# How the negated score maxima get from partitions into rows, and where early score tiles stand, in a fused layernorm, attention and gated MLP kernel

## The chip, the cores and the metric

One core of one Trainium2 chip runs the whole kernel as a single program. The metric is device time in microseconds, from the program's start to its end. The kernel before took 1572.92 us in the median of three runs (1572.62 to 1572.99).

The engines are named as the profile names them. PE is TensorE (PEld is its weight load, which overlaps its products), DVE is VectorE, ACT is ScalarE, POOL is GpSimd, and SP is SyncE, which here only issues DMAs. SPq and PEq are the instruction queues of SP and PE.

## What is computed

The input `x` has 2048 tokens of 512 features. All is float32.

```python
xn = layernorm(x)
q, k, v = split(xn @ wqkv)              # 32 heads of 16 features
scores = einsum("bhqd,bhkd->bhqk", q, k) * 16 ** -0.5
p = softmax(scores, axis=-1)
s = einsum("bhqk,bhkd->bhqd", p, v).reshape(1, 2048, 512) @ wo
g = silu(gelu(xn @ w1 + b1) @ w2 + b2)  # 1376 hidden features
out = x + s * g
```

The softmax subtracts each row's maximum, so every query of every head needs the maximum of its 2048 scores before its exponentials are taken. This study is about the way of these maxima through the kernel.

## The kernel before

**Precision.** Products are made in float32r, and where full accuracy is needed an operand is split into a high part and a low rest, so that one product becomes three (high by high, high by low, low by high). The attention scores do this inside one product: the 48 rows of a K tile and of a Q tile hold the 16 features of a head three times, as high, high and low, against high, low and high.

**Units and steps.** The attention is cut into 32 units: 8 groups of 4 heads by 4 chunks of 512 queries; unit `u` has group `u // 4` and chunk `u % 4`. A unit has 16 steps, one for each 128 keys, so there are 512 steps (the loop of line 975). A step is a short program of letters, `ORDER` and `AFTER` (lines 40 and 41), most often `TSXTTSTYV`:

- T (`t_one`, line 709) is the score tile of one head, 128 keys by 512 queries. Its product has 50 rows: the 48 of the features and two more, in which the K side holds ones and the Q side, `QT[u]`, holds the negated maxima as a high and a low part. So the maximum is subtracted inside the product (line 716). ACT takes the exponential from PSUM (line 718). A step has four Ts, and their PSUM banks come from `t_tile` (line 701): three of `ps_t` and the one of `ps_m` in turn.
- V (`pv_step`, line 775) multiplies the exponentials of the step before by V; a column of ones in V gives the sums. After a unit's sixteenth step DVE copies the result out (line 788).
- S, X and Y are score tiles made only for their maxima, 128 queries by 512 keys, for a unit that comes later. Their banks are a ring of three in the attention (two before it). DVE takes the maxima of each half of 256 keys (line 190). X and Y are the two halves of a tile cut in two.

**The early phase.** Before the attention, layernorm, the projections of Q, K and V and the MLP are computed. Most of it is a list called `plan`, whose products run on two halves of the PE array, 64 rows each: `run` (line 595) takes two lists of products and issues them in turn, one for the upper and one for the lower rows. Ahead of each product it calls `fill(a)` (line 564), which may put in one early score tile. `LEAD = 144` makes 576 early score tiles, the maxima of units 0 to 8; they use the banks `ps_a` and `ps_b` in turn. A tile of half `a` is due when the row counter of that half, which counts products and early tiles of that half, reaches

```python
due = FILL0 + put[0] + sum(made) * ROWS // (4 * LEAD)    # line 565; ROWS is 1728, so 3 for each tile made
```

Since the two halves have counters of their own and take turns, the tiles stand seven products apart, then three, then seven.

**How a unit's maxima are finished.** After 64 tiles `s_end0` (line 239) joins the maxima of all key parts: `nm` holds, for 128 queries on the partitions, 16 negated maxima (4 heads by 4 query tiles) (line 248, DVE). `s_max` (line 187) calls it right after the reduction of the next score tile, so in the attention it stands where that tile happens to stand in its step. POOL makes the high and the low part (lines 251 and 252) into `nmh`. The maxima now lie on the partitions, one query on each, and have to become rows of `QT[u]`. For this a product with the identity transposes them into PSUM (`s_end1`, line 268), for two units at once up to unit 27 and for one unit at a time after it (`PAIRED`, line 43). Its bank is one of the score tiles' ring in the early phase and one of the T ring in the attention, but for the last unit. A copy brings it to SBUF (`s_end2`: ACT in the early phase, line 276, DVE in the attention, line 278), and SP writes it to DRAM (line 279) as `mh_d`, in which a head's 512 maxima are one run. `load_mh` (line 149) then reads them with two DMAs of 8 KB, each into two rows of `QT[u]`.

`tick`, `flush` and the list `later` count score tiles or steps until line 268 is put in (12 in the early phase, 8 in the attention, where a step counts four).

**Order of the work around it.** All orders are written out by hand (`manual_schedule`): an engine runs its instructions in the order in which the Python code makes them. `at(n, ...)` (line 925) puts an operation into step `n`. Unit `u`'s rows of Q are loaded at step `16 * u - 14`, and `load_mh` stands at that step too, or four steps after the unit's pair has all its tiles if that is later (two steps for the last unit) (lines 944 to 946). `o_move` and `o_den` (lines 798 and 807), which carry a finished unit's result and sums, stand on the same SP queue. SP's DMAs share eight completion semaphores in turn, so each waits until the one eight before it has landed.

Of the kernel before, what the change touches and what calls it, by code (L numbers as in the profile page):

```python
# [8 lines left out]
F32 = mybir.dt.float32  # L9
F32R = mybir.dt.float32r  # L10
# [39 lines left out]
def fused(ctx: ExitStack, tc: tile.TileContext, x, wqk, wv, wo, w1, b1, w2, b2, out):  # L50
# [13 lines left out]
    ones_d = dpool.tile([2, S], F32, name="ones_d")  # L64
    g_d = dpool.tile([S, D], F32, name="g_d")
    den_d = dpool.tile([NG * NCH, GH, CH], F32, name="den_d")
    mh_d = dpool.tile([NG * NCH, 2, GH, CH], F32, name="mh_d")

    ident_r = keep.tile([P, P], F32R, name="ident_r")
    mhw = keep.tile([1, 1], F32, name="mhw")  # L70
# [12 lines left out]
            if then:  # L83
                then()

    QS, QT, MX, NM, MH = {}, {}, {}, {}, {}
# [62 lines left out]
    def load_mh(u):  # L149
        assert u in sent  # L150
        for a in range(2):
            nc.sync.dma_start(QT[u][64 * a + 48:64 * a + 50].bitcast(F32), mh_d[u, :, a::2, :])
# [6 lines left out]
    def units_of(u):  # L159
        return (u,) if u >= PAIRED else (u - u % 2, u - u % 2 + 1)  # L160

    def tick():
        for e in later:
# [23 lines left out]
    def s_max(ps, job, heads, parts):  # L187
        u, p = job[0], job[2]
        qi, ki = at_of(job)
        nc.vector.tensor_reduce(MX[u][:, 2 * p:2 * p + 2, qi, ki][:, heads, parts], ps.rearrange("p (n c) -> p n c", c=HC), axis=AX.X, op=OP.max)  # L190
        done[u] += 1
        if ended:
            s_end0(ended.pop())
        if done[u] == 64:
            ended.append(u)
        if done[NU - 1] == 64:
            s_end0(ended.pop())

    def s_whole(job, a):
        ps = s_tile()[0]  # L200
# [4 lines left out]
        made[a] += 1  # L205
        s_whole(heads[made[a] - 1], a)

    jobs, whole, cut, put_off = [], [], [], []

    def s_op(op):  # L210
        if op == "S":
            if whole:
                s_whole(whole.pop(), 1)
            else:
                whole.append(jobs.pop(0))
                s_whole(whole[0], 0)
        elif op == "X":
            if not cut:
                cut[:] = [jobs.pop(0), 0]
            ps, pool = s_tile(True)  # L220
            x = s_mm(ps, cut[0], 0, 0, cut[1] * HC, HC)
            cut[2:] = [ps, pool, x]
            run_off()
# [11 lines left out]
    def run_off():  # L235
        while put_off:
            put_off.pop(0)()

    def s_end0(u):
        nm = qring.tile([P, GH * NCH], F32, name="nm")  # L240
        n = len(units_of(u))
        if u == units_of(u)[0]:
            NM[u] = qring.tile([P, 2, 2, GH * NCH], F32R, name="nmh")[:, :n]
        hl = NM[units_of(u)[0]][:, u % n]
        if u == units_of(u)[-1]:
            later.append([12 if "seen" in prog else 8, units_of(u)[0]])
        mx = MX.pop(u).rearrange("p a b c n -> p (a b) (c n)")
        nc.vector.tensor_reduce(nm, mx, axis=AX.X, op=OP.max, negate=True)  # L248

        def two():  # L250
            nc.gpsimd.tensor_copy(hl[:, 0], nm)  # L251
            nc.gpsimd.tensor_sub(hl[:, 1], nm, hl[:, 0].bitcast(F32))

        put_off.append(two)
        if "seen" in prog or u == NU - 1:
            run_off()
        del QS[u]
        if "seen" in prog:
            ask_qs(u + 2)
        else:  # L260
            load_qs(u + 2)

    prog = {}

    def s_end1(u):
        pm = s_tile()[0] if "seen" in prog or u == NU - 1 else t_tile()
        n = 2 * GH * NCH * len(units_of(u))
        nc.tensor.matmul(pm[:n, :P], NM.pop(u).rearrange("p u i a -> p (u i a)"), ident_r, start=True, stop=True)
        MH[u] = pm

    def s_end2(u):
        us = units_of(u)
        n = 2 * GH * NCH * len(us)
        mh = qring.tile([4 * GH * NCH, P], F32, name="mh", bufs=1)
        if "seen" in prog:
            nc.scalar.activation(mh[:n], MH.pop(u)[:n, :P], AF.Copy)
        else:
            nc.vector.tensor_copy(mh[:n], MH.pop(u)[:n, :P])
        nc.sync.dma_start(mh_d[us[0]:us[-1] + 1].rearrange("u i j (q s) -> (u i j q) s", s=P), mh[:n])
        sent.update(us)  # L280

    sa = ExitStack()
    xp = sa.enter_context(tc.tile_pool(name="xp", bufs=1))
# [273 lines left out]

    prog.update(n=0, pe=0, seen=0)
    writer = {}
    s_when, put, row = [], [0], [0, 0]  # L560
    ndown = sum(1 for e in plan if e[0] == "down")
    ROWS = 12 * (4 * VQ + 2 * len(pairs)) + 6 * ndown - 10 + 2 * LEAD - 2 * (LEAD // 32) - FILL0

    def fill(a):
        due = FILL0 + put[0] + sum(made) * ROWS // (4 * LEAD)
        if sum(made) < 4 * LEAD and row[a] >= due and (made[0] <= made[1]) == (a == 0):
            taken()
            if later and later[0][0] <= 0:
                put[0] += 2
                u = later.pop(0)[1]  # L570
                s_end1(u)
                s_end2(u)
                return
            s_one(a)
            row[a] += 1
            tick()

    def taken():
# [5 lines left out]
    def mm(a, key, ps, lhs, rhs, first, last):  # L584
        r = slice(64 * a, 64 * a + 64)
        if not first and writer[key][0] != a and writer[key][1] > prog["seen"]:
            hold = nc.tensor.nop().ins
            tc.add_manual_dep(hold, writer[key][2], SYNC, reason="other row tile")
            prog["seen"] = writer[key][1]
        i = nc.tensor.matmul(ps, lhs[r], rhs[r], start=first, stop=last).ins  # L590
        prog["pe"] += 1
        row[a] += 1
        writer[key] = (a, prog["pe"], i.name)

    def run(ops, hooks={}):
# [335 lines left out]
    def due(n):  # L931
        return min(4 * L, 4 * LEAD + max(0, 3 * n - 1))

    for u in range(NU):
# [116 lines left out]
```

## Time and profile before

| | |
|---|---|
| median of 3 runs | 1572.92 us |
| profiled execution | 1573.31 us |
| span of its instructions | 1571.4 us |
| PE, DVE, ACT, POOL busy | 1564.2, 1397.1, 1233.8, 371.9 us |
| granted TensorE clock | 1.00 |
| layernorm and start | to about 52 us |
| early phase, two halves of the array | about 52 to 475 us |
| attention, 512 steps | about 473 to 1548 us |
| output projection, what is left of it | to the end |

The profiled execution took 1.9 us more than its span and 0.39 us more than the median. In the profile a line such as L268 is a line of the kernel before. A group gives its busy time and the mean of one instruction, and then the idle time of its engine just ahead of it and what ended that. In the timeline the first column is the start in us from the span's start and the second the duration; equal neighbours are merged (x8). In the windows each engine's busy time is followed by its number of instructions. In a DMA answer the strip is the window in 40 equal slices, each digit the share of 16 DMA engines that was busy, in tenths.

### The profile page before, as it was taken

To read this page: it belongs to the slowest core of one execution; us is meant where nothing else is said; L and a number is where in the kernel's file an instruction comes from. 1 tells how busy PE (TensorE), PEld (TensorE's weight loads), DVE (VectorE), ACT (ScalarE), POOL (GpSimd) and SP (SyncE) were. 2 spreads that over 40 slices of the span, in tenths; PEclk is the share of its full clock that TensorE was granted. 3 is DMA by queue.
4 is the path that set the end of the run, shared out by engine and by line. 5 is a ranking of instruction groups with operands and counts; after the bars stand their busy time and mean duration, and the time that the engine had idled before them with its cause. 6 is when DMAs were issued, how large, how long until landed. Compare 5 with 4: busy or idle time off the path is not lost.

```text
span 1571.4 us, 31849 instructions
## 1 busy us (share of the span) xinstructions
PE 1564.2 (100%) x12264; PEld 952.0 (61%) x12264; DVE 1397.1 (89%) x2290; ACT 1233.8 (79%) x2397; POOL 371.9 (24%) x394
## 2 busy tenths in 40 slices
PE   9999999999999999999999999999999999999998
PEld 7899999999994444444444444444444444444455
DVE  7599898989988999999999999999999999999834
ACT  4333333333339999999999999999999999999984
POOL 4145575766741001001100100100010000000143
PEclk9999999999999999999999999999999999999999
DMA  6626343454322114111511511321061111110163
GB/s 208 152 59 150 122 139 99 141 152 120 131 84 75 42 30 71 32 36 38 82 32 32 69 33 40 51 52 29 21 81 29 33 29 31 42 30 22 45 199 111
DMA packets 74648, 116.87 MB, mean 74 GB/s; under 512 B 23013, under 2 KB 24293, under 8 KB 73321
## 3 DMA queue, kind: packets, MB, share of 16 engines
q1 hardware_dynamic: 70748, 101.89, 24.1%
q0 software_dynamic: 3264, 12.35, 4.7%
q8 instruction: 97, 1.59, 0.4%
q10 hardware_dynamic: 484, 0.60, 0.1%
q14 instruction: 55, 0.44, 0.1%
HBM read 84.35 MB, written 25.97 MB: 70 GB/s over the span
## 4 chain that ended last, share of the span: by engine, by line
PE 98%; DVE 1%; ACT 0%; DMA 0%; issue 0%; DVEq 0%
PE pv L781 33%; PE pst L716 20%; PE ps L590 13%; PE ps L184 12%; PE pst L590 7%; PE ps L716 6%; PE pv L590 2%; PE ps L905 1%; PE ps L81 1%; PE ps L459 1%; PE pst L81 1%; DVE st L418 0%; PE pst L441 0%; DMA xt<-in_x 0%; PE pst L459 0%
## 5 line engine op out<-in xcount | busy, mean ns | idle before, releaser
L190 DVE TENSOR_REDUCE mx<-ps 128x2 f32<-128x512 f32 x2048 | 1298.8, 685 | 113.7 <-PE ps L184 45.5
L718 ACT ACTIVATE slot<-pst 128x512 f32<-128x512 f32 x1533 | 826.0, 603 | 14.0 <-PE pst L716 7.5
L781 PE MATMUL pv<-slot,vsb 128*32 128x512 f32 x4096 | 545.3, 605 | 0.3 <-DVE os L788 0.3
L716 PE MATMUL pst<-qt,kt 50*128 50x512 f32 x1149 | 380.3, 430 | 0.6 <-DVE gt L649 0.4
L184 PE MATMUL ps<-kt,slot 48*128 48x512 f32 (+1 forms) x1364 | 377.4, 367 | 0.0
L716 PEld LDWEIGHTS pst<-qt,kt 50*128 50x128 f32 x1149 | 191.6, 184 | 256.8 <-ACT slot L718 240.4
L718 ACT ACTIVATE slot<-ps 128x512 f32<-128x512 f32 x515 | 310.9, 604 | 1.9 <-PE ps L184 0.5
L184 PEld LDWEIGHTS ps<-kt,slot 48*128 48x128 f32 x1364 | 225.5, 184 | 40.3 <-DVE mx L190 35.2
L590 PE MATMUL ps<-slot,w1h 64*128 64x512 f32 x1088 | 217.8, 393 | 0.0
L184 PE MATMUL ps<-kt,qz 48*128 48x512 f32 x512 | 213.7, 417 | 0.0
L184 PE MATMUL ps<-slot,slot 48*128 48x512 f32 (+1 forms) x598 | 165.7, 366 | 0.0
L716 PE MATMUL ps<-qt,kt 50*128 50x512 f32 x387 | 160.0, 416 | 0.0
L590 PEld LDWEIGHTS ps<-slot,w1h 64*128 64x128 f32 x1088 | 154.4, 185 | 4.6
L590 PE MATMUL ps<-slot,w1l 64*128 64x512 f32 x544 | 142.0, 393 | 0.0
L781 PEld LDWEIGHTS pv<-slot,vsb 128*32 128x32 f32 x4096 | 80.7, 108 | 100.3 <-issue 92.3
L378 POOL TENSOR_TENSOR hl<-hg,hh 128x512 fp32r<-128x512 f32 x76 | 96.8, 1296 | 151.5 <-ACT hh L377 99.7
L371 ACT ACTIVATE hg<-ps,b_sb 128x512 f32<-128x512 f32 x44 | 27.8, 684 | 132.7 <-PE ps L590 116.9
L251 POOL CAST nmh<-nm 128x16 fp32r<-128x16 f32 x32 | 6.3, 196 | 489.1 <-DVE nm L248 466.6
L716 PE MATMUL pst<-qt,slot 50*128 50x512 f32 x384 | 111.3, 415 | 0.0
L184 PEld LDWEIGHTS ps<-slot,slot 48*128 48x128 f32 x598 | 98.8, 184 | 17.2 <-DVE mx L190 15.2
L184 PEld LDWEIGHTS ps<-kt,qz 48*128 48x128 f32 x512 | 93.7, 183 | 18.7
L716 PEld LDWEIGHTS ps<-qt,kt 50*128 50x128 f32 x387 | 71.1, 184 | 37.5 <-ACT slot L718 31.9
(165 smaller groups left out, 1715.7 us busy)
## 6 DMA issues: line engine op xcount, KB each, us to landing
raw<-in_w SPq DMA_DIRECT2D x88, 256.0 KB
qk_h<-hh SPq DMA_DIRECT2D x32, 256.0 KB
qk_l<-hl SPq DMA_DIRECT2D x32, 256.0 KB
qt<-qk_h SPq DMA_DIRECT2D x128, 64.0 KB
slot<-qk_h SPq DMA_DIRECT2D x92, 64.0 KB
g_d<-gt POOLq DMA_DIRECT2D x16, 256.0 KB, 3.5
qt<-qk_l SPq DMA_DIRECT2D x64, 64.0 KB
dn<-den_d SPq DMA_DIRECT2D x32, 128.0 KB
```

The source lines that it names most:

```text
L81: nc.tensor.matmul(ps, lhs[a], rhs[b], start=first and n == 0, stop=last and n == 2)
L184: return nc.tensor.matmul(ps[:, c0:c0 + w], QS[u][r, p, qi * P:(qi + 1) * P], kts[u // NCH % KB][p][r, k0:k0 + w], start=True, stop=True).ins
L190: nc.vector.tensor_reduce(MX[u][:, 2 * p:2 * p + 2, qi, ki][:, heads, parts], ps.rearrange("p (n c) -> p n c", c=HC), axis=AX.X, op=OP.max)
L251: nc.gpsimd.tensor_copy(hl[:, 0], nm)
L371: nc.scalar.activation(raw, ph.pop(u), AF.Gelu_apprx_tanh, bias=b1_sb[:, u[2]:u[2] + 1])
L378: nc.gpsimd.tensor_sub(hl, raw, hh.bitcast(F32))
L459: nc.tensor.matmul(pq["q", g, c], W1[g][i][:, k * P:(k + 1) * P], (xh, xl)[j][c][:, k], start=n == 0 and k == 0, stop=n == 2 and k == KT - 1)
L590: i = nc.tensor.matmul(ps, lhs[r], rhs[r], start=first, stop=last).ins
L716: nc.tensor.matmul(ps, kts[g % KB][p][r, k * P:(k + 1) * P], QT[u][r, p, :], start=True, stop=True)
L718: nc.scalar.activation(PT[u, k][:, 2 * p + a, :], ps, AF.Exp, scale=SCALE)
L781: nc.tensor.matmul(PV[u][32 * j:32 * j + 32, :], vsb[:, k, h:h + 32], PT[u, k][:, j, :], start=(k == 0), stop=(k == NT - 1))
L905: HALF[0] = nc.tensor.matmul(PW[i][0], OTS[i, k][x][r], (wo_h, wo_l)[y][r, k], start=k == 0 and side == 0 and n == 0, stop=k == KT - 1 and ...
```

## The change

It has three parts.

1. **No transposition on PE.** `s_end1`, `s_end2`, `units_of`, `PAIRED`, `put_off` and the tiles behind them go. POOL writes the high and low parts of a unit into `nmh` in another order of its columns, and `s_send` writes the 32 numbers of each of 128 queries to DRAM as they lie: `mh_d[u]` has a run of 128 bytes for each query. `load_mh` makes the transposition: four DMAs for a unit, each into one row of `QT[u]`, 1024 numbers, which it picks out of `mh_d[u]` one by one, 128 bytes apart. Every unit goes alone.
2. **The joining is moved.** In the attention `s_end` (the old `s_end0`) is called ahead of a step's first T, in the first step after the unit's tiles are complete whose number in its unit is 3 or more (any step for the last unit). In the early phase it comes, as before, after the next score tile. The write follows eight ticks later (four for the last unit), `load_mh` seven steps after completion at the earliest (two for the last unit).
3. **Early score tiles five apart.** One counter of the products of both halves decides. The tiles stand exactly five products apart, beginning after 60 products as before, and nothing else takes a turn of their ring.

```diff
+APART = 5
-PAIRED = 28
-    mh_d = dpool.tile([NG * NCH, 2, GH, CH], F32, name="mh_d")
+    mh_d = dpool.tile([NG * NCH, P, 2, 2, GH * NCH // 2], F32, name="mh_d")
     def load_mh(u):
         assert u in sent
         for a in range(2):
-            nc.sync.dma_start(QT[u][64 * a + 48:64 * a + 50].bitcast(F32), mh_d[u, :, a::2, :])
+            for i in range(2):
+                r = 64 * a + 48 + i
+                nc.sync.dma_start(QT[u][r:r + 1].bitcast(F32).rearrange("o p (q s) -> o (p q) s", s=P),
+                                  mh_d[u:u + 1, :, i, a].rearrange("o s j -> o j s"))
...
         done[u] += 1
-        if ended:
-            s_end0(ended.pop())
         if done[u] == 64:
             ended.append(u)
-        if done[NU - 1] == 64:
-            s_end0(ended.pop())
...
-    def s_end0(u):
+    def s_end(u):
+        ended.remove(u)
+        NM[u] = qring.tile([P, 2, 2, GH * NCH // 2], F32R, name="nmh")
+        later.append([8 if u < NU - 1 else 4, u])
         nm = qring.tile([P, GH * NCH], F32, name="nm")
...
         nc.vector.tensor_reduce(nm, mx, axis=AX.X, op=OP.max, negate=True)
-        def two():
-            nc.gpsimd.tensor_copy(hl[:, 0], nm)
-            nc.gpsimd.tensor_sub(hl[:, 1], nm, hl[:, 0].bitcast(F32))
-        put_off.append(two)
-        if "seen" in prog or u == NU - 1:
-            run_off()
+        nm = nm.rearrange("s (p a q) -> s a p q", p=2, a=2)
+        hi, lo = [NM[u][:, i].rearrange("s a (p q) -> s a p q", p=2) for i in range(2)]
+        nc.gpsimd.tensor_copy(hi, nm)
+        nc.gpsimd.tensor_sub(lo, nm, hi.bitcast(F32))
...
+    def s_send(u):
+        nc.sync.dma_start(mh_d[u], NM.pop(u).bitcast(F32))
+        sent.add(u)
-    def s_end1(u):
-        pm = s_tile()[0] if "seen" in prog or u == NU - 1 else t_tile()
-        n = 2 * GH * NCH * len(units_of(u))
-        nc.tensor.matmul(pm[:n, :P], NM.pop(u).rearrange("p u i a -> p (u i a)"), ident_r, start=True, stop=True)
-        MH[u] = pm
-    def s_end2(u):
...
     def fill(a):
-        due = FILL0 + put[0] + sum(made) * ROWS // (4 * LEAD)
-        if sum(made) < 4 * LEAD and row[a] >= due and (made[0] <= made[1]) == (a == 0):
+        due = 2 * FILL0 + APART * sum(made)
+        if sum(made) < 4 * LEAD and row[0] >= due and (made[0] <= made[1]) == (a == 0):
             taken()
-            if later and later[0][0] <= 0:
-                put[0] += 2
-                u = later.pop(0)[1]
-                s_end1(u)
-                s_end2(u)
-                return
+            flush()
+            ready = list(ended)
             s_one(a)
-            row[a] += 1
+            for u in ready:
+                s_end(u)
             tick()
...
-        row[a] += 1
+        row[0] += 1
...
-            need = min(n for n in range(L) if due(n) >= 64 * (units_of(u)[-1] + 1)) + (4 if u < NU - 1 else 2)
+            need = min(n for n in range(L) if due(n) >= 64 * (u + 1)) + (7 if u < NU - 1 else 2)
             at(max(16 * u - 14, need), load_mh, u)
...
         i = 0
+        for u in list(ended) if 2 < ka or u == NU - 1 else ():
+            s_end(u)
         order = ORDER[want] if n > 1 else ("TTTTV", "TTSTSVT")[n]
```

More of the change, by code (lines that the diff above doesn't have):

```diff
@@ L84, in mm3 @@
                 then()
-    QS, QT, MX, NM, MH = {}, {}, {}, {}, {}
+    QS, QT, MX, NM = {}, {}, {}, {}
     SYNC = mybir.DependencyInfo(mybir.DependencyClass.Sync, mybir.DependencyReason.DATA)
@@ L157, in fused @@
     later, ended, errands, sent = [], [], [], set()
-    def units_of(u):
-        return (u,) if u >= PAIRED else (u - u % 2, u - u % 2 + 1)
     def tick():
@@ L167, in flush @@
         while later and later[0][0] <= 0:
-            u = later.pop(0)[1]
-            run_off()
-            s_end1(u)
-            s_end2(u)
+            s_send(later.pop(0)[1])
     def at_of(job):
@@ L206, in s_one @@
         s_whole(heads[made[a] - 1], a)
-    jobs, whole, cut, put_off = [], [], [], []
+    jobs, whole, cut = [], [], []
     def s_op(op):
@@ L222, in s_op @@
             cut[2:] = [ps, pool, x]
-            run_off()
         else:
@@ L559, in fused @@
     writer = {}
-    s_when, put, row = [], [0], [0, 0]
-    ndown = sum(1 for e in plan if e[0] == "down")
-    ROWS = 12 * (4 * VQ + 2 * len(pairs)) + 6 * ndown - 10 + 2 * LEAD - 2 * (LEAD // 32) - FILL0
+    s_when, row = [], [0]
     def fill(a):
-        due = FILL0 + put[0] + sum(made) * ROWS // (4 * LEAD)
-        if sum(made) < 4 * LEAD and row[a] >= due and (made[0] <= made[1]) == (a == 0):
+        due = 2 * FILL0 + APART * sum(made)
+        if sum(made) < 4 * LEAD and row[0] >= due and (made[0] <= made[1]) == (a == 0):
             taken()
-            if later and later[0][0] <= 0:
-                put[0] += 2
-                u = later.pop(0)[1]
-                s_end1(u)
-                s_end2(u)
-                return
+            flush()
+            ready = list(ended)
             s_one(a)
-            row[a] += 1
+            for u in ready:
+                s_end(u)
             tick()
```

19 lines of the change are left out of this document (removed).

## The prediction, on record before the changed kernel ran

> **What bounds the kernel now.** I read the page's span and chain of waits first, then the windows of the two long stages, then who waited for whom.
>
> ```profile
> span 1571.4 us, 31849 instructions
> PE 98%; DVE 1%; ACT 0%; DMA 0%; issue 0%; DVEq 0%
> ```
> ```profile
> core 0: us, PE busy (x) PEld busy (x) DVE busy (x) ACT busy (x) POOL busy (x), PEclk, DMA share, GB/s
> 73.00:473.00 400.00, 400.00 (x3365) 367.13 (x3364) 360.19 (x565) 141.79 (x259) 232.97 (x205) 1.00 0.41 118
> 473.00:1560.00 1087.00, 1086.13 (x8418) 518.82 (x8416) 984.25 (x1610) 1062.32 (x2082) 113.97 (x159) 1.00 0.23 50
> ```
> ```profile
> PEld pst L716 <- ACT slot L718: 271.4, 325, 0.8
> ```
>
> The chain is PE's, but a modelled PE is always busy, so it tells little. The early phase (first window) has PE full and DVE at 90%: products bound it, score tiles follow closely. In the attention (second window) ACT is at 98% and PE's weight loads wait 271.4 us for ACT's exponentials: four exponentials a step set the pace, and whatever keeps a T's bank, or delays a step, is paid in full. So the change is worth what single operations push these two rhythms out of step, and it costs what the new loads make late. The sum is made against the profiled run, 1573.31 us, which is 0.39 us over the median of 1572.92.
>
> **Joining and transposing in the attention.** V's first weight load marks each step. Timeline of PE's weight loads, and of DVE, around three joinings:
>
> ```profile
> 565.66 0.16 PEld L781 LDWEIGHTS pv<-slot,vsb 128*32 128x32 f32 x8 [0.20 <-issue]
> 567.88 0.16 PEld L781 LDWEIGHTS pv<-slot,vsb 128*32 128x32 f32 x8 [0.25 <-issue]
> 569.88 0.16 PEld L781 LDWEIGHTS pv<-slot,vsb 128*32 128x32 f32 x8 [0.16 <-issue]
> 571.95 0.16 PEld L781 LDWEIGHTS pv<-slot,vsb 128*32 128x32 f32 x8 [0.21 <-issue]
> ...
> 613.20 0.16 PEld L781 LDWEIGHTS pv<-slot,vsb 128*32 128x32 f32 x8 [0.25 <-issue]
> 614.20 0.13 PEld L268 LDWEIGHTS pst<-ident_r,nmh 128*64 128x64 f32 x1 [0.84 <-issue]
> 615.41 0.16 PEld L781 LDWEIGHTS pv<-slot,vsb 128*32 128x32 f32 x8 [0.16 <-issue]
> ...
> 652.29 0.16 PEld L781 LDWEIGHTS pv<-slot,vsb 128*32 128x32 f32 x8 [0.21 <-issue]
> 654.30 0.16 PEld L781 LDWEIGHTS pv<-slot,vsb 128*32 128x32 f32 x8 [0.16 <-issue]
> ```
> ```profile
> 565.80 0.28 DVE L248 TENSOR_REDUCE nm<-mx 128x16 f32<-128x128 f32 x1
> ...
> 653.59 0.28 DVE L248 TENSOR_REDUCE nm<-mx 128x16 f32<-128x128 f32 x1
> ```
>
> An undisturbed step is (571.95 - 567.88) / 2 = 2.035 us. With line 248 amid a step (565.80) it took 567.88 - 565.66 = 2.22 us, 0.18 more. With line 248 between the last reduction of one step and the first of the next (653.59) it took 654.30 - 652.29 = 2.01 us: nothing. With the transposition (614.20) it took 615.41 - 613.20 = 2.21 us, 0.18 more.
>
> How many? A unit ends every 21.3 steps, so completions fall, in turn, at steps 6, 11 and 1 of a unit (step 22, 43, 65, ...). Those at 6 are the free ones; those at 11 and 1 are joined amid a step. Units 9 to 30 have 7 of each costly kind: 14 joinings. The change puts all at the head of a step, where 653.59 shows them free (those at 1 are moved to step 3, off the steps with the copy of V's result). I take 0.16 each, a little under the 0.18: 14 x 0.16 = **2.2 us**. Ends: 0 (the head of other steps is no better) and 2.5.
>
> ```profile
> L278 DVE COPY mh<-pst x9: 273/280/283, 614.5 to 1405.0; 64x128 f32<-64x128 f32 x7, 32x128 f32<-32x128 f32 x2
> L278 DVE COPY mh<-ps x5: 269/273/283, 523.8 to 1492.2; 64x128 f32<-64x128 f32 x3, 32x128 f32<-32x128 f32 x2
> L276 ACT ACTIVATE mh<-ps x4: 255/270/270, 159.1 to 434.7; 64x128 f32<-64x128 f32 x4
> ```
>
> By the copies there are 9 + 5 = 14 transpositions in the attention and 4 in the early phase. In the attention each takes a turn of the four banks of T until DVE has copied it; 14 x 0.18 = **2.5 us** go. Ends: 1.2 (half of it comes back, as T's banks keep another rhythm) and 3.5.
>
> **Transposing in the early phase.** A window without a transposition and one with (at 250 us):
>
> ```profile
> 220.00:240.00 20.00, 20.00 (x172) 18.43 (x169) 18.13 (x29) 7.02 (x13) 11.16 (x10) 1.00 0.36 119
> 240.00:260.00 20.00, 20.00 (x168) 17.82 (x167) 17.40 (x29) 6.98 (x14) 8.91 (x10) 1.00 0.34 102
> ```
>
> 172 products in 20 us are 0.116 us each. The second window has four fewer, and one of its 168 is the transposition, so five others, 5 x 0.116 = 0.58 us, are lost. A window's edge is good for one product, so I take 0.5: 4 x 0.5 = **2.0 us** go. Ends: 1.4 (three products) and 2.4.
>
> **Five apart.** Reductions of early tiles, the weight load of one early tile, and products of the same stage ahead of the first early tile:
>
> ```profile
> 198.89 1.29 DVE L190 TENSOR_REDUCE mx<-ps 128x2 f32<-128x512 f32 x2
> 200.34 2.70 DVE L190 TENSOR_REDUCE mx<-ps 128x2 f32<-128x512 f32 x4 [0.16 <-PE pst L590]
> 203.22 2.68 DVE L190 TENSOR_REDUCE mx<-ps 128x2 f32<-128x512 f32 x4 [0.18 <-PE ps L590]
> 206.06 0.69 DVE L190 TENSOR_REDUCE mx<-ps 128x2 f32<-128x512 f32 x1 [0.16 <-PE pst L590]
> ```
> ```profile
> 200.23 0.18 PEld L184 LDWEIGHTS ps<-kt,qz 48*128 48x128 f32 x1
> ```
> ```profile
> 54.50 2.92 PE L590 MATMUL pst<-kt,slot 64*128 64x512 f32 x24
> 57.25 0.39 PE L590 MATMUL pv<-kt,slot 64*128 64x512 f32 x1
> ```
>
> Four tiles and their twenty products take (206.06 - 200.34) / 2 = 2.86 us; 24 products alone took 57.25 - 54.50 = 2.75. So 0.11 of each four tiles is waiting, 144 x 0.11 = 16 us in all. But the load at 200.23 follows the reduction that ended at 198.89 + 1.29 = 200.18: tiles wait for one of two banks. A bank's round is its product, its reduction and two handovers, and equal distances shorten none of these; they only spare the 0.16 that DVE loses when a tile comes late after seven products, and PE must fill that at the same time. I take **1.5 us**, near the end at which nothing changes; ends: a loss of 6 (0.02 more for each pair of 288 tiles) and a gain of 16.
>
> **The new loads.** Off PE, ACT and DVE the change adds DMAs on SP. The write of 128 runs per unit is a few tenths of a microsecond on SP, hidden unless somebody waits. `load_mh` becomes 4 DMAs of 1024 runs of 4 bytes. Before, no data packet is that small. The nearest are 128 packets of 64 bytes; the far end is the mean of all packets of the queue:
>
> ```profile
> DMA  0000001255868675556575444332110010000000
> DMA packets 144, 0.01 MB, mean 28 GB/s; under 512 B 144, under 2 KB 144, under 8 KB 144
> q1 hardware_dynamic: 144, 0.01, 30.9%
> ```
> ```profile
> q1 hardware_dynamic: 70748, 101.89, 24.1%
> ```
>
> In that 0.3 us window a packet took 0.309 x 16 x 300 / 144 = 10.3 ns of an engine; where the strip is fullest, 80%, that is 13 ns a packet, and over its 27 busy slices (0.2 us, 9 packets an engine) 22. The mean packet, 1.4 KB, took 0.241 x 16 x 1571.4 us / 70748 = 86 ns. I take 13, nearest in size, where engines are kept fed. The source of each load has an outer loop of 8 rows of 128 numbers; I take one engine a row, so a unit has 4 x 128 = 512 packets in line: 6.7 us (16 engines: half of it). The Trainium skill ("DMA: Bandwidth & Descriptors", section "Queues, rings and completion order" and its part on why a DMA adds 16) has the engines as the largest number up to 16 that divides both slowest loops, which is 8 here too; no run here shows it yet.
>
> Who waits? Most units' loads are issued 14 steps ahead, 28 us, and cover is ample up to 50 ns a packet. The last two are near:
>
> ```profile
> 1488.16 0.22 POOL L252 TENSOR_TENSOR nmh<-nm,nmh 128x16 fp32r<-128x16 f32 x1
> ```
> ```profile
> 1450.76 1.35 SPq L152 DMA_DIRECT2D qt<-mh_d  x2
> ...
> 1492.53 0.33 SPq L279 DMA_DIRECT2D mh_d<-mh  x1
> 1493.97 1.37 SPq L152 DMA_DIRECT2D qt<-mh_d  x2
> ```
> ```profile
> DMA  0000000000000000000800000020000070000072
> ```
> ```profile
> 1462.32 0.18 PEld L716 LDWEIGHTS pst<-qt,kt 50*128 50x128 f32 x1
> ...
> 1499.46 0.18 PEld L716 LDWEIGHTS pst<-qt,kt 50*128 50x128 f32 x1 [0.84 <-ACT slot L718]
> ```
>
> For the last unit the write no longer waits for PE and DVE (1492.53) but only for POOL, done at 1488.38: write at 1488.5, loads 1.44 later (1493.97 - 1492.53), at 1489.9. The strip, 1494.5 to 1496.5 in 40 slices, has the first packet in slice 20, near 1495.4, 1.45 us after its issue; so packets from 1491.4 and the end at 1491.4 + 6.7 = 1498.1, ahead of the unit's first T at 1499.46. **No wait**, with 1.4 us to spare; it is used up at (1499.46 - 1491.4) / 512 = 15.7 ns a packet. Unit 30's loads stand on SP where they stood (1450.76), behind the reciprocal sums: 1452.2 + 6.7 = 1458.9, T at 1462.32; used up at 19.8 ns. Queued behind the loads on SP are Q rows, the sums' way through DRAM and, at the end, the gate's inputs; these have seven steps, and the last ones three.
>
> **Nothing** for the rest: POOL's other column order, the later joining of unit 8, the two more DMAs of a unit on SP. POOL is busy 114 of 1087 us in the attention and SP waits between units.
>
> **Sum:** 2.2 + 2.5 + 2.0 + 1.5 = 8.2 us. 1573.3 - 8.2 = 1565.1; on the median's scale, 0.39 less, **1564.7**. Parts at their low ends without loss give 1570.3, at their high ends 1548.5.
>
> **Rivals.**
>
> - *Late maxima (slower).* Packets of 4 bytes read one by one from DRAM cost more than 13 ns, and PE waits for `QT` ahead of unit 31 and, from 19.8 ns, unit 30. At 22 ns: 3.2 + 1.1 = 4.3 us, 1569. The gain of 8.2 is eaten at 1024 p - 18.2 = 8.2, p = 26 ns; a measurable loss begins at 29 ns; at 33 ns the time is 1580, at 40 ns 1587, and above 50 ns every unit's loads are late, by hundreds of microseconds at 86. For it: no small reads in the trace, and the 22 of the strip. Against it: 10.3 ns busy, and nothing in a 4-byte packet to move. The same page of the Trainium skill (section "Rules for kernel authors") speaks against such loads: a strided last dimension becomes one descriptor for each element, and a plain DMA that rearranges is put 19 times behind the hardware's transposition. That is this rival's mechanism; its section "Bandwidth" has about 10.5 ns a packet for small transfers that GpSimd issues, by which, as an estimate, 512 take 5.4 us and nobody waits.
> - *Tiles five apart gain in full.* The waits vanish, 16 us instead of 1.5: 1550. For it: DVE's 0.16 gaps; against it: the bank's round.
> - *Five apart loses.* Both tiles of a pair meet the bank's round, a loss of 6 us where 1.5 were gained: 1572.
> - *The joining moves but isn't free.* Every one of 23 costs 0.16: 2.2 lost, 1.5 more: 1568.4.
>
> **Chances.** Forecast with its parts within their ends (1560 to 1569.5): 0.54. Five apart in full: 0.06. Joining not free: 0.05. Late maxima, 22 to 29 ns (1569 to 1576): 0.11; above 29 ns: 0.19. Five apart loses: 0.05. What a measurement can tell from no change is 0.2%, 3.1 us. Faster (below 1569.8): 0.54 + 0.06 + 0.05 = 0.65; slower (above 1576.1): 0.19 and 0.02 of mixtures, 0.21; within: 0.14. The range leaves out 0.06 below 1557 and the worst of late maxima, 0.14, above 1580.
>
> **What would show it.** Right: no step longer than 2.1 us at a joining; windows of 20 us in the early phase all with some 172 products or more; unit 31's first T without a wait for the loads of `mh_d`; 4096 packets of 4 bytes a unit at 10 to 15 ns. Wrong: a wait of PE's T for a DMA, steps of 2.2 us at units' steps 3, 7 and 12, or fewer products in 20 us than 171.

## The result, and the profile after

The changed kernel takes **1686.81 us** in the median of 5 runs (1683.22 to 1690.09), against 1572.99 us (1572.62 to 1573.60) for the kernel before on the same chip: a ratio of 1.073, 95% interval 1.071 to 1.074. That is 114 us slower, where 8 us faster was forecast, and outside the range.

The page of the changed kernel: its span, its DMA queue (packets, MB, share of 16 engines) and the chain of waits.

```profile
span 1681.4 us, 31947 instructions
...
q1 hardware_dynamic: 205756, 101.89, 49.0%
...
PE 65%; DMA 19%; SPq 8%; ACT 4%; issue 2%; DVE 1%; POOL 1%; ACTq 0%; POOLq 0%
```

Before, the chain was PE's by 98% and the queue had 24.1% of the engines for the same 101.89 MB. Now DMA and SP's queue hold 27% of the chain, and the queue takes more than twice the engine time. Who waited for whom tells where:

```profile
PEld ps L678 <- ACT slot L680: 386.0, 454, 1.7
...
PEld ps L678 <- issue: 95.8, 12, 15.7
...
PE ps L678 <- DMA qt<-mh_d: 66.1, 12, 14.8
...
PE ps L678 <- DMA mh_d<-nmh: 22.1, 2, 13.7
```

Line 678 is T's product (line 716 before). It still waits for ACT in most steps, but twelve times for the loads of the maxima, up to 14.8 us, and twice, by the profile's account, for a write of maxima. These two are waits for the loads as well, as unit 8 shows below. The twelve waits of the weight load, for which the profile names nobody, are the same waits seen a moment earlier, and are not to be added. The windows of the stages, with the columns of the prediction's windows:

```profile
73.00:473.00 400.00, 392.57 (x3362) 367.32 (x3359) 379.62 (x565) 142.52 (x257) 234.89 (x206) 1.00 0.45 119
473.00:1560.00 1087.00, 1013.47 (x7705) 475.45 (x7709) 935.48 (x1527) 982.14 (x1925) 77.52 (x129) 0.96 0.58 38
220.00:240.00 20.00, 20.00 (x176) 19.11 (x174) 19.42 (x31) 7.03 (x13) 11.78 (x11) 1.00 0.35 122
240.00:260.00 20.00, 20.00 (x176) 18.46 (x174) 19.57 (x30) 7.66 (x14) 11.98 (x10) 1.00 0.43 128
```

The two 20 us windows have 176 products each, where there were 172 and 168: the early phase runs faster than forecast. It loses that at its end (392.57 of 400 us busy), and in the attention PE is idle for 74 of 1087 us, at a granted clock of 0.96.

Unit 8 shows one of the waits. POOL's K loads, then SP's queue, then PE:

```profile
756.43 1.06 POOL L110 DMA_DIRECT2D kt<-qk_h  x2 [0.26 <-issue]
...
758.95 0.50 POOL L110 DMA_DIRECT2D kt<-qk_l  x1
```
```profile
758.72 23.57 SPq L154 DMA_DIRECT2D qt<-mh_d  x4
782.39 5.78 SPq L135 DMA_DIRECT2D slot<-qk_h  x1
```
```profile
781.41 0.50 PE L181 MATMUL ps<-kt,slot 48*128 48x512 f32 x1
795.65 0.76 PE L678 MATMUL ps<-qt,slot 50*128 50x512 f32 x1 [13.75 <-DMA mh_d<-nmh]
```

The four loads for unit 9 were issued at 758.7, their issue alone held SP for 23.6 us, and PE stood until 795.65. That is 37 us from issue to use, and 14 steps give 28. The write that the profile names was issued at 793.66, behind the loads, and shares a completion semaphore with the third of them. By the updates of the semaphores in the trace the four loads had landed at 782.0, 787.9, 793.6 and 795.5 us, and PE went on at 795.6.

### The profile page after: what moved, and what is told of

It is laid out like the page before. It is cut to its first block, busy times and chain, and to the rows that moved or that the text cites. A ratio compares the mean times of both kernels' runs of the same rounds, so it can differ in the third digit from the quotient of the medians.

```text
span 1681.4 us, 31947 instructions
## 1 busy us (share of the span) xinstructions
PE 1579.9 (94%) x12246; PEld 961.6 (57%) x12246; DVE 1417.1 (84%) x2276; ACT 1233.4 (73%) x2393; POOL 372.5 (22%) x394
## 3 DMA queue, kind: packets, MB, share of 16 engines
q1 hardware_dynamic: 205756, 101.89, 49.0%
## 4 chain that ended last, share of the span: by engine, by line
PE 65%; DMA 19%; SPq 8%; ACT 4%; issue 2%; DVE 1%; POOL 1%; ACTq 0%; POOLq 0%
PE pv L743 19%; DMA qt<-mh_d 18%; PE ps L552 10%; PE pst L678 8%; PE ps L181 8%; PE ps L678 7%; PE pst L552 6%; SPq L154 6%; ACT slot L680 4%; SPq L135 2%; PE pv L552 2%; PE ps L867 1%; PE ps L81 1%; PE ps L427 1%; PE pst L81 1%
## 5 line engine op out<-in xcount | busy, mean ns | idle before, releaser
L187 DVE TENSOR_REDUCE mx<-ps 128x2 f32<-128x512 f32 x2048 | 1320.2, 687 | 168.5 <-PE ps L181 114.0
L680 ACT ACTIVATE slot<-pst 128x512 f32<-128x512 f32 x1533 | 803.6, 604 | 1.4 <-PE ps L678 0.7
L678 PE MATMUL pst<-qt,kt 50*128 50x512 f32 x1149 | 306.5, 407 | 0.1
L678 PE MATMUL ps<-qt,kt 50*128 50x512 f32 x387 | 194.2, 504 | 66.4 <-DMA qt<-mh_d 50.9
L678 PEld LDWEIGHTS pst<-qt,kt 50*128 50x128 f32 x1149 | 210.7, 188 | 19.0 <-DVE mx L187 0.8
L181 PE MATMUL ps<-kt,qz 48*128 48x512 f32 x512 | 201.7, 394 | 0.0
L552 PE MATMUL ps<-slot,w1l 64*128 64x512 f32 x544 | 158.0, 392 | 0.0
L781 POOL TENSOR_TENSOR ot<-ot,dn 64x512 f32<-64x512 f32 x15 | 19.2, 1278 | 399.7 <-DMA dn<-den_d 322.0
L678 PE MATMUL pst<-qt,slot 50*128 50x512 f32 x384 | 100.7, 409 | 0.0
L678 PEld LDWEIGHTS ps<-qt,slot 50*128 50x128 f32 x128 | 23.9, 187 | 126.3 <-ACT slot L680 98.1
```

Of the source, the lines that this page charges most:

```text
L181: return nc.tensor.matmul(ps[:, c0:c0 + w], QS[u][r, p, qi * P:(qi + 1) * P], kts[u // NCH % KB][p][r, k0:k0 + w], start=True, stop=True).ins
L678: nc.tensor.matmul(ps, kts[g % KB][p][r, k * P:(k + 1) * P], QT[u][r, p, :], start=True, stop=True)
L680: nc.scalar.activation(PT[u, k][:, 2 * p + a, :], ps, AF.Exp, scale=SCALE)
L781: eng.tensor_mul(ot[c][rs, g // 2], ot[c][rs, g // 2], DN.pop(u)[rs])
```

## The experiments

They ask which part of the change costs, and by what mechanism. My forecast had the theory that a 4-byte packet occupies a DMA engine for some 13 ns and that eight engines share them. The rivals after the result: the packets cost more wherever they go; they cost more because of where they land; or it isn't the packets, but the place of the loads behind others.

In several of them I compare V's first weight load of unit 0 (the end of the early phase) and of unit 31 (the end of the attention at full pace): 476.86 and 1505.14 us in the kernel before, 480.15 and 1615.69 after.

**1. Early tiles five apart, alone** (on the kernel before).

```diff
-        due = FILL0 + put[0] + sum(made) * ROWS // (4 * LEAD)
-        if ... row[a] >= due ...
-                put[0] += 2
+        due = 2 * FILL0 + put[0] + APART * sum(made)
+        if ... row[0] >= due ...
+                put[0] += APART
...
-            row[a] += 1
...
-        row[a] += 1
+        row[0] += 1
```

> The kernel before with early tiles five products apart and nothing else; the four transpositions stay in the early phase, each in a turn of the tiles' ring. Theory that the spacing pays more than I forecast: the changed kernel had 3114 products where the kernel before had 3057 between 73 and 433 us, 57 more at 0.116 us, 6.6 us; less 2.0 us for its four transpositions, 4.6 us remain for the spacing: 1568.4 us. My forecast of the spacing (1.5 us): 1571.5 us. Rival, that the missing transpositions made it all: no gain, 1573 us.

Measured: 1566.45 us (before: 1572.76), ratio 0.996 [0.994, 0.997]; unit 0 begins at 471.16 instead of 476.86, **5.7 us earlier**. DVE's timeline of this kernel, in the stretch where the prediction showed gaps:

```profile
197.72 9.85 DVE L191 TENSOR_REDUCE mx<-ps 128x2 f32<-128x512 f32 x14
```

Fourteen reductions follow each other without a gap, 9.85 / 14 = 0.704 us each, 2.81 for four, where four with their products took 2.86. The spacing pays by itself, and more than I gave it.

**2. The maxima read as they lie** (on the changed kernel; this leaves out the transposition, and the factor of the exponential is 1e-6).

```diff
-    nc.sync.dma_start(QT[u][r:r + 1]...rearrange("o p (q s) -> o (p q) s", s=P), mh_d[u:u + 1, :, i, a].rearrange("o s j -> o j s"))
+    nc.sync.dma_start(QT[u][r:r + 1]...rearrange("o p c -> o (p c)"), mh_d[u:u + 1, i, 64 * a:64 * a + 64].rearrange("o s a j -> o (s a j)"))
...
```

The layout of `mh_d` changes with it, and the write makes two runs of 64 bytes for each query instead of one of 128.

> The changed kernel, but its four loads of a unit each read 4 KB as they lie in DRAM: same bytes, same rows, same queue and place, no packet of 4 bytes. The transposition is left out, so the maxima are in a wrong order, and the factor of the exponential is 1e-6 so that it can't overflow. Theory that the 4-byte packets alone cost the time: the rest of the change is left, 6.6 us in the early phase and 0.16 us in each of 26 units (units 6, 10, 18 and 22 of the changed kernel took 32.87 us in the mean, 0.16 less than before), 4.2 us: 1562 us. Rival, that the place or number of the loads (four for a unit on SP, each unit alone, issued behind the K loads) costs it: 1600 us or more, with PE still waiting for them at units 8, 12, 16 and 20.

Measured: 1560.68 us, ratio 0.992 [0.991, 0.994]. The four loads of a unit stand where they stood and bring as many bytes into the same rows; the packets of 4 bytes are gone, and with them 1686.81 - 1560.68 = **126 us**. The rival of place and number falls. What is left of the change is worth 12.1 us.

**3. Ten forms of loads by themselves.**

> Not the kernel: ten forms of loads, each alone, with a wait for its landing before the next; the output is zeros. a: one load of 1024 numbers, 128 bytes apart, into partition 48. b: four of them into partitions 48, 49, 112, 113, as in the changed kernel. c: the same in the order 48, 112, 49, 113. d: four of 1024 numbers into 8 neighbouring partitions. e: four into all 128 partitions. f: four of 4 KB as they lie. g: as b with 512 pieces of 8 bytes. h: one write of 4096 numbers to DRAM, 4 bytes each, then f. i: four with numbers that lie together, put 8 bytes apart in one partition. j: as d, but into partitions 0, 4, ... 28. One partition takes a number each 5.6 ns: a 5.7 + 2, b 23 + 2, c 23, i 23, g 12 us, but d and j and e a few us. Slow reads of 4 bytes: a, b, c, d, e and j all alike for their number, i short. A price per packet on the engines: a, b, c, d, e, i, j alike and h as long as b.

In its timeline each form's issue on SP is followed by DVE's instruction that waited for the landing (forms a, b, d, i, j in turn):

```profile
14.05 0.83 SPq L51 DMA_DIRECT2D qt<-mh_d  x1
21.17 0.15 DVE L39 COPY mark<-qt 128x1 f32<-128x1 f32 x1 [8.85 <-DMA qt<-mh_d]
...
22.54 12.17 SPq L55 DMA_DIRECT2D qt<-mh_d  x4
47.65 0.15 DVE L39 COPY mark<-qt 128x1 f32<-128x1 f32 x1 [20.86 <-DMA qt<-mh_d]
...
77.21 4.41 SPq L63 DMA_DIRECT2D big<-mh_d  x4
86.75 3.47 DVE L42 MEMSET big<- 128x4096 f32 x1 [8.30 <-issue]
...
130.93 2.67 SPq L85 DMA_DIRECT2D big<-mt_d  x4
155.25 3.47 DVE L42 MEMSET big<- 128x4096 f32 x1 [23.09 <-issue]
...
158.75 4.07 SPq L90 DMA_DIRECT2D big<-mh_d  x4
165.95 3.47 DVE L42 MEMSET big<- 128x4096 f32 x1 [5.96 <-DMA big<-mh_d]
```

| form | numbers | into | issue to landing |
|---|---|---|---|
| a, 128 bytes apart in DRAM | 1024 | one partition | 7.1 us |
| b, as in the changed kernel | 4096 | four, one after the other | 25.1 us |
| c, order 48, 112, 49, 113 | 4096 | four, one after the other | 22.6 us |
| i, together in DRAM, 8 bytes apart in SBUF | 4096 | four, one after the other | 24.3 us |
| d, as b | 4096 | eight neighbours at once | 9.5 us |
| j, as b | 4096 | 0, 4, ... 28 at once | 7.2 us |
| f, runs of 4 KB | 4096 | four, one after the other | 2.4 us |
| h, write to DRAM | 4096 | DRAM, 4 bytes each | 17.8 us |

The landing is taken at the instruction that waited for it. By the updates of the semaphores the last number came 0.1 us earlier in a, b, c and h, but 1.0 us earlier in d, i and j, which so took 8.5, 23.3 and 6.2 us; f's time is by the semaphores alone.

b and j read the same numbers from the same places with the same number of DMAs; only the landing differs, 25.1 against 7.2 us. i reads numbers that lie together and is about as slow as b. So the reads are not what costs: **into one partition goes about one 4-byte number in 6 ns** ((25.1 - 7.1) / 3072 = 5.9 ns). The DMA views of b, j and i in turn, cut from issue to landing:

```profile
DMA  0026599999999000026419000004400000000000
...
DMA packets 4128, 0.02 MB, mean 1 GB/s; under 512 B 4128, under 2 KB 4128, under 8 KB 4128
...
q1 hardware_dynamic: 4128, 0.02, 57.3%
```
```profile
DMA  0000000004577617737504467700577730000000
...
q1 hardware_dynamic: 4128, 0.02, 32.0%
```
```profile
DMA  0055998999999000000002100000000000000000
...
q1 hardware_dynamic: 4160, 0.02, 81.6%
```

These shares add up the times of packets, and each packet's whole time is put into the slice in which it begins. So the empty slices behind the nines are not idle engines. Nor is a share a count of engines: i's packets add up to 0.816 x 16 x 24.32 = 318 us, and ran from 132.2 to 145.9, 13.7 us, in which 16 engines have 219. An engine can have more than one packet in hand. In j a packet takes 0.320 x 16 x 7.20 us / 4128 = 8.9 ns in the mean, in b 0.573 x 16 x 25.11 / 4128 = 56 ns. Three of four packets of b took 9 ns too, and the longest 4.4 us: the engines stand with packets in hand (nines in the strip, at 1 GB/s) until these are taken. The Trainium skill ("DMA: Bandwidth & Descriptors", section "Back-pressure in remote DMA") says, of DMAs between cores, that a saturated destination port of SBUF clogs the path back to the engines; this agrees with it inside one core. In d, with eight neighbouring partitions, a packet took 15.6 ns in the mean and the longest 1.2 us, where none of j took over 9 ns. So neighbours hinder each other, and the limit isn't the single partition's alone; what they share, these runs don't show. Form e came out as pieces of 32 bytes and tells nothing; g (2048 pieces of 8 bytes) landed within 14.5 us, partly beside h.

**4. The transposition in the write** (on the changed kernel).

```diff
-        nc.sync.dma_start(mh_d[u], NM.pop(u).bitcast(F32))
+        nc.sync.dma_start(mh_d[u].rearrange("i a j s -> s (i a j)"), NM.pop(u)...)
...
```

`mh_d` is laid out as [u, i, a, j, s] here, and the four loads read runs of 4 KB.

> The changed kernel with the transposition in the write instead of the load: one DMA of 4096 numbers from 128 partitions to DRAM, 4 bytes each, then four loads of 4 KB runs. Theory that one partition takes numbers one after the other, 5.6 ns each (180 a microsecond in the changed kernel's trace, whatever the number of engines): writes come from all partitions and go to DRAM, so this limit is gone, 4096 packets at 9 ns on 16 engines are 2.3 us, and the time is that of the rows as they lie, 1562 us, plus 2 us or so at the last unit: 1564 us. Rival, that each 4-byte packet costs an engine 45 to 85 ns wherever it goes: 12 to 22 us for a unit's write, hidden for most units but not for the last two: 1585 us or more.

Measured: 1617.27 us, ratio 1.028 [1.026, 1.030]. My theory failed here: no number lands in a crowded partition, and yet the write takes 17.8 us (form h), the length that the rival gave, though not "wherever it goes" (form j). 50 of the 62 us over the profile of the maxima read as they lie (1621.0 against 1559.0) came ahead of the attention, where the early phase's weights stand behind such writes (with the maxima read as they lie, ACT waited 10.0 and 8.0 us for these loads):

```profile
ACT w1h L265 <- DMA raw<-in_w: 93.9, 25, 14.1
...
ACT w1h L265 <- DMA raw<-in_wqk: 59.7, 11, 13.1
```

In the attention, only units 29 and 30 were late, by 3.2 and 7.4 us.

**5. The joining at the head of a step, alone** (on the kernel before).

```diff
-        if ended:
+        if ended and "seen" in prog:
             s_end0(ended.pop())
...
+        if ended and (2 < ka or n == 0):
+            s_end0(ended.pop())
         order = ORDER[want] ...
```

> The kernel before with the joining moved to the head of a step in the attention, and nothing else. My forecast for this part, 14 joinings at 0.16 us: 2.2 us, 1570.6 us. With the maxima read as they lie, the attention up to unit 31 was 3.65 us shorter than before (1024.63 against 1028.28 us) by this part and the missing transpositions together; if the joining isn't free at the head, the transpositions made all of it and the time stays at 1572.8 us.

Measured: 1572.28 us (before: 1573.08), ratio 0.9996 [0.9986, 1.0005], no difference that the timing shows. By the traces the attention from unit 0 to unit 31 is 1027.45 instead of 1028.28 us, 0.8 less. By units: those in which line 248 stood at step 1 (units 8, 16) fell from 32.92 to 32.76 us, as forecast; those with step 6 (9, 17), which I had taken as free, rose by 0.08 and 0.05; those with step 11 (10, 18) fell by 0.03.

**6. Spacing and joining, with the transposition left on PE** (edits of 1 and 5 together).

> The kernel before with early tiles five apart and the joining at the head of a step: the change without its third part, the maxima are still transposed on PE. If the parts add up: 1566.5 us (spacing alone) less 2.2 us: 1564.3 us, faster than both kernels. Rival, that the joining gains nothing by itself: 1566.5 us.

Measured: 1566.06 us, ratio 0.996 [0.994, 0.997]; 0.4 us less than the spacing alone, which the timing can't tell from nothing. The rival named the time. By the traces the attention from unit 0 to unit 31 fell from 1028.29 to 1027.52 us, 0.8 as in experiment 5.

**7. K loads behind the loads of maxima** (on the changed kernel).

```diff
-                at(64 * (g - KB + 1) + 6 + i, load_k, g, (i,), nc.gpsimd)
+                at(64 * (g - KB + 1) + 6 + i, load_k, g, (i,), nc.sync)
```

> The changed kernel with the K loads of groups 4 to 7 issued on SP instead of POOL, six steps after the unit's loads of maxima, so that they stand behind them. In the changed kernel the six K pieces were issued at 756.4 to 759.5 us, the loads of maxima at 758.7, and their packets began only at 771. Theory that units 8, 12, 16 and 20 are late because K's 1.5 MB came first: their 16.3, 10.7, 15.5 and 16.3 us over the kernel before shrink to the 1 us of their neighbours, about 55 us less in all, 1632 us; the last units' waits stay. Rival, that 4-byte packets collide with whatever is on the engines: the same 1687 us, with the waits after K instead.

Measured: 1686.04 us in one run. Units 8, 12 and 16 lost their waits, and unit 20 most of its (32.69, 32.70, 32.92 and 36.77 us instead of 49.20, 43.82, 48.46 and 49.36), as the theory had it, but units 9, 13, 17 and 21 took them over (45.61, 47.93, 50.79, 46.27). The total came out as the rival had it, for another reason. SP's queue:

```profile
757.78 10.54 SPq L154 DMA_DIRECT2D qt<-mh_d  x4
...
779.19 0.77 SPq L110 DMA_DIRECT2D kt<-qk_h  x2
...
789.03 0.59 SPq L775 DMA_DIRECT2D dn<-den_d  x1
789.67 0.92 SPq L110 DMA_DIRECT2D kt<-qk_h  x2
...
803.37 10.62 SPq L154 DMA_DIRECT2D qt<-mh_d  x4
```

Unit 9 began at 783.6, so its successor's loads were due two steps later, near 788; they were issued at 803.37, behind the K pieces and what waited among them. So a load of 25 us has 3 us to spare in the 28 of its cover, and whatever comes ahead of it is paid.

**8. Half of the 4-byte reads** (on the changed kernel; the rows of low parts are left in another order).

```diff
+                if i:
+                    nc.sync.dma_start(QT[u][r:r + 1]..., mh_d[u:u + 1, 64 * a:64 * a + 64, i]...)
+                    continue
```

> The changed kernel with only the two rows of high parts put together from 4-byte reads, 2048 for a unit instead of 4096; the two rows of low parts are read in 32-byte pieces as they lie, so their order is wrong. Theory, one partition takes a number each 6.0 ns, so a unit's loads are 12 us shorter, and only what exceeds this cover comes through: against the maxima read as they lie, the changed kernel was over by 16.4, 11.0, 15.7 and 16.6 us at units 8, 12, 16 and 20, by 11.4 and 16.5 at 29 and 30, by 11.8 before the attention, and by 5.5 or less elsewhere; less 12 each and nothing below zero, 4.4 + 3.7 + 4.6 + 4.5 = 17 us stay: 1578 us. Rival, that the waits come from queueing behind other transfers and not from the count of numbers: half of the packets changes little, 1680 us; a rival in which time falls with the count, without a cover: half of 126 us, 1624 us.

Measured: 1576.60 us (1573.64 to 1585.29), ratio 1.002 [1.001, 1.004]. The pieces were of 64 bytes, not 32. The profile is of the longest of ten executions (span 1583.5); its excess over the maxima read as they lie stands at units 8, 12, 16, 20 and 30, with 6.4, 4.3, 3.4, 4.5 and 5.5 us, and 0.1 ahead of the attention. The places are the expected ones and unit 12, which was to be free. Half the numbers cost an eighth of the time: price by count, less a cover.

**9. The same reads, turned first** (on the changed kernel: into 32 partitions of a tile, eight steps ahead, back to DRAM, and from there in long runs; the last unit over PE).

```diff
...
+    def s_turn(u):
+        HOP[u] = qring.tile([2 * GH * NCH, P], F32, name="hop", bufs=1)
+        nc.sync.dma_start(HOP[u], mh_d[u].rearrange("s i a j -> (i a j) s"))
+    def s_back(u):
+        nc.sync.dma_start(mt_d[u].rearrange("i a (j s) -> (i a j) s", s=P), HOP.pop(u))
     def load_mh(u):
+        for a in range(2):
+            nc.sync.dma_start(QT[u][64 * a + 48:64 * a + 50]..., mt_d[u, :, a])
...
```

> The changed kernel with the same 4096 reads of 4 bytes for a unit, but into 32 partitions of a tile of their own, eight steps ahead, from there to DRAM in 512-byte runs and then into the two pairs of rows with two loads; the last unit is transposed on PE. Theory that the slow part is one partition that takes numbers one after the other (25 us for four rows of one partition each, 7 us for the same number into eight partitions): no unit waits, and the time is that of the maxima read as they lie, 1561 us, up to 1563 with the last unit's way over PE. Rival, that 4096 reads of 4 bytes cost as much wherever they land: 20 us or more for each, SP's queue is held for it, 1600 us or more.

Measured: **1560.91 us** (1560.57 to 1561.02), ratio 0.992 [0.991, 0.994]: faster than both kernels, by 12 and 126 us. SP's timeline, and the queue's line of the page:

```profile
716.85 0.45 SPq L153 DMA_DIRECT2D hop<-mh_d  x1
722.00 0.32 SPq L156 DMA_DIRECT2D mt_d<-hop  x1
```
```profile
q1 hardware_dynamic: 202780, 102.91, 29.5%
```

The second DMA needs the first one's data, so 4096 reads of 4 bytes landed within 722.00 - 716.85 = 5.2 us. With the maxima read as they lie, the same line is

```profile
q1 hardware_dynamic: 78012, 101.89, 24.1%
```

so 124768 packets more took (0.295 - 0.241) x 16 x 1559.1 us = 1347 us of packet time, 10.8 ns each. In the changed kernel 127744 more took 0.490 x 16 x 1681.4 - 0.241 x 16 x 1559.0 = 7171 us, 56 ns each. Nearly the same packets, another landing.

## Why the prediction was wrong

Its parts, with what the runs showed (a gain is negative):

| step | forecast (ends) | measured | by |
|---|---|---|---|
| joining at the head | -2.2 (0 to -2.5) | -0.8 | experiment 5, attention 1028.28 to 1027.45 us |
| no transposition in the attention | -2.5 (-1.2 to -3.5) | -2.8 | experiments 6 and 9, 1027.52 to 1024.73 us |
| no transposition in the early phase | -2.0 (-1.4 to -2.4) | -2.2 | experiments 6 and 9, unit 0 at 470.76 and 468.55 us |
| five apart | -1.5 (+6 to -16) | -5.7 | experiment 1, unit 0 at 476.86 and 471.16 us |
| new loads | 0 | +126 | experiment 2 against the changed kernel |

**The step that failed** is the new loads: "I take 13, nearest in size, where engines are kept fed ... one engine a row, so a unit has 4 x 128 = 512 packets in line: 6.7 us". As the price of a packet that nothing holds up 13 ns was near (10.8 in experiment 9), and the eight engines were right (below). But the rows for it, 64-byte packets, said nothing of many packets into one partition, and I took the number of engines as the only thing in line. A unit's loads take 25 us, four rows of 1024 numbers at 6 ns, and by my sum that would be 25.1 / 512 = 49 ns a packet. The rule of the Trainium skill that I had weighed ("DMA: Bandwidth & Descriptors", "Rules for kernel authors": a strided last dimension becomes one descriptor for each element) held as a warning, for form b took 25.1 us and form f 2.4; the estimate from the same page's price for a small packet, 5.4 us, missed like mine.

The rival of late maxima had the wait, PE's for `QT`, and 0.30 of the chance, but it put the price on reading from DRAM one by one. At 49 ns its 1024 p - 18.2 gives 32 us for the loads of units 30 and 31; their waits fall into units 29 and 30, which lost 11.4 and 16.5, 28 in all. It said that "above 50 ns every unit's loads are late", and at 49 most units indeed just pass (units 5 to 25 without K loads lost 0 to 1.3 us). What it left out is what else lies in the 28 us of cover. Against the maxima read as they lie the changed kernel's 1681.4 - 1559.0 = 122.4 us of span stand here:

| where | us |
|---|---|
| ahead of unit 0 (loads issued at 450.7, used at 475.2) | 11.8 |
| units 3, 4, 8, 12, 16, 20, in which K is loaded | 67.0 |
| units 27 to 30 | 34.1 |
| all other units | 9.9 |
| after unit 31 begins | -0.2 |

More than half is the K loads, whose 1.5 MB shares the engines with the loads of maxima. "Cover is ample" was worked out for the loads alone. I listed what stands behind them on SP and not what goes ahead of them on the engines, and I didn't ask where unit 0's loads stand, which have no attention step ahead of them.

**Five apart** had the right sign, and a size too small by four. I argued that "a bank's round is its product, its reduction and two handovers, and equal distances shorten none of these", and let only DVE's 0.16 count. In the stretch of experiment 1 no gap is left. My reading is that a tile that comes late after seven products makes the next ones late at DVE; no run takes this apart. My figure for the round, 16 us of waiting in 144 rounds, was the right bound to weigh; a third of it went.

**The joining** was read from one free row (653.59) and one dear one (565.80). The dear place at step 1 is cured by 0.16, as taken; the one at step 11 wasn't dear (0.03), and the free one at step 6 became dear. The two **transpositions** came out as taken, and the parts without the loads at 12.1 us (experiment 2) where 8.2 were forecast.

Of what should show it, the windows held (174 products or more in each 20 us from 60 to 460 us), and so did the steps at a joining (2.00 to 2.12 us up to unit 29). One sign for wrong came: T waited for the loads, 66.1 and 22.1 us. And a packet took 56 ns where 10 to 15 should have shown.

## What to carry to other kernels

Before a DMA rearranges by single elements, ask where the elements land: many numbers into one partition stand in line there whatever the number of engines, while the same reads into 32 partitions, and long runs from there, cost a few microseconds. A load's cover has to be counted with all that shares the engines at that moment, and every place without cover (the first and the last unit) has to be looked at by itself. Take the parts of a change apart early: here the parts that I had priced were worth 12 us together, and the one that I had put at zero took them ten times over.

## What the runs showed of the hardware

- Four loads of 1024 numbers hold SP's queue for 12.2 us by themselves (22.54 in the ten forms), and 23.6 us at 758.72 in the changed kernel: what stands behind them on SP isn't even issued.
- 4096 4-byte writes into DRAM took 17.8 us (form h).
- A single load of 1024 numbers is taken from the engines long before it lands. Form a, from its issue at 14.05 to its landing:

```profile
DMA  1000000006437720000000000000000000000000
...
q1 hardware_dynamic: 1048, 0.01, 8.4%
```

  Its packets, 9.1 ns each (0.084 x 16 x 7.12 us / 1048), are over by slice 15 of 40, near 16.7 us; it landed at 21.17. So some thousand numbers wait behind the engines, and the engines are held only when more come, as in b.
- One such load runs on eight engines, as I had taken with the Trainium skill ("DMA: Bandwidth & Descriptors", the part on why a DMA adds 16), and the trace agrees: form a's semaphore has one update at 15.27 us and then eight, from 20.75 to 21.07. b and j have 4128 packets, 4 x 8 more than numbers; i, whose slowest loop is 1024, has 4160, 4 x 16 more, and is hardly faster for its sixteen engines. The 70% in two slices of form a's strip count packets and not engines.
- A wait costs more than its length. V's first weight load around the wait at unit 8, and the windows in and behind it (the seventh figure is the granted clock):

```profile
780.41 0.16 PEld L743 LDWEIGHTS pv<-slot,vsb 128*32 128x32 f32 x8 [0.19 <-issue]
797.41 0.20 PEld L743 LDWEIGHTS pv<-slot,vsb 128*32 128x32 f32 x8 [0.44 <-issue]
801.03 0.16 PEld L743 LDWEIGHTS pv<-slot,vsb 128*32 128x32 f32 x8 [0.41 <-DVE mx L187]
```
```profile
785.00:794.00 9.00, 0.00 (x0) 0.00 (x0) 0.00 (x0) 0.00 (x0) 0.00 (x0) 0.50 0.55 30
```
```profile
798.00:800.00 2.00, 2.00 (x12) 0.63 (x6) 1.18 (x2) 0.52 (x2) 0.61 (x1) 0.50 0.05 9
800.00:802.00 2.00, 2.00 (x16) 0.78 (x12) 1.84 (x4) 1.89 (x4) 0.00 (x0) 0.76 0.20 63
```

PE stood idle, its clock fell to 0.50, and the step after the wait took 3.62 us instead of 2.04; the clock was back between 800 and 802. The Trainium skill ("TensorE: Matmul & The Clock Gate", "Part 1: The HAM clock gate") has the array at half its clock after about 3.4 us of idleness; the trace agrees with the half.
